# Decode attention on one core: V ahead of the output projection, and eight V rows in small loads

## The chip, the cores and the metric

One NeuronCore of a Trainium2 chip. The metric is the device time of one execution in microseconds, the median of several runs.

## The reference

One token passes through attention over a cache of 65,536 positions and through a gated MLP, and a scalar gate mixes the two:

```python
# x [1,1,512] bf16; k_cache, v_cache [1,32,65536,128] bf16; wq [512,4096]; wo [4096,512]
# w_gate, w_up [512,1792]; w_down [1792,512]; gate_w [512]
q = (x @ wq).reshape(1, 1, 32, 128).transpose(0, 2, 1, 3)
scores = einsum("bhqd,bhkd->bhqk", q, k_cache) * 128 ** -0.5
o = einsum("bhqk,bhkd->bhqd", softmax(scores), v_cache)
a = o.transpose(0, 2, 1, 3).reshape(1, 1, 4096) @ wo
b = (silu(x @ w_gate) * (x @ w_up)) @ w_down
g = sigmoid((x * gate_w).sum(-1, keepdims=True))
return g * a + (1 - g) * b
```

K and V are 537 MB each and are read once. The weights are some 14 MB.

## The kernel before

All loads go into one large buffer, `mem`, of 184 units; a unit is 512 bf16 columns in 128 partitions, 128 KB. A head's 65,536 positions are cut into two halves (z = 0 and 1), and in each half a partition holds 256 consecutive positions, "rows" of 128 elements here. So a half of K or V is 64 units, 8 MB, one DMA. K's halves lie at units 32 to 95 and 0 to 63, V's at 120 to 183 and 96 to 159: they overlap, so a load waits until what it overwrites has been used.

SP issues nearly all loads, in an order written out by hand. Inside its loop over heads: K's first half of head i+2, V's first half of head i+1, K's second half, V's second half. Each waits on one of two counters: `ktdone` counts K pieces that DVE has transposed, `pvdone` the groups of V matmuls that PE has finished.

For a head, DVE transposes K in 16 pieces of 32 rows (L415, L422) into the two buffers of `kt`. PE makes scores from each piece (L472), into `psS`. The maximum of the scores goes through DVE and PE, ACT takes the exponentials into `pa` (L288), and DVE rearranges them into the coefficients `pb` (`shuffle`, L331; signals `s_pba` and `s_pbz` for the two halves). PE then makes four rows of partial sums in `psO` with matmuls of four V rows each, 128x512 (`values`, L525), in four groups per head of 40, 24, 40 and 24 matmuls. ACT scales the four rows into `orow`, and `turn` (L499) adds and turns them into a column in `psT`, which ACT stores in `oTn`. PE runs one head behind: in the loop's iteration i it makes the scores of head i and the values of head i-1. Before, the order in an iteration is: six pieces of K's first half, the first 40 V matmuls, the last two pieces, `turn`, 24 V matmuls, the eight pieces of K's second half, 40 V matmuls, 24 V matmuls.

Behind the loop is the last head's V, in eight loads of `tail`, each entry a place in `mem`, a first row and a number of rows. `piece` (L561) uses every V row as weights, with one column of coefficients, and adds into the column `psW`. The output projection wo is applied in three parts: 31 of its 32 rows per partition (`wo`, loaded ahead of V's tail) by 31 matmuls of 128x512 into `psY` (L576), which already holds the MLP's result; row 31 (`wj`) for the other heads, and the last head's block (`w31`) for the head that has just been finished, both loaded last, by eight matmuls of 128x128 into `psZ` (L600). `psY` reaches `psZ` through `yrow` and `hot` (L584). ACT copies `psZ` to `fin`, and SP and ACT store two of the four output rows each.

The MLP, the gate and q are made at the start, while the first K loads run.

## Time and profile before

| | before |
|---|---|
| median of 3 runs | 2513.8 us (2513.74 to 2513.82) |
| span of the profiled execution | 2512.4 us |
| PE, DVE, ACT busy | 1709.8, 1411.8, 64.6 us |
| bytes read from HBM | 1087.77 MB, 433 GB/s over the span |
| packets on SP's DMA queue | 20452 |

The profile is of one execution. The span runs from its first to its last instruction, and it is the only time that the profile gives of this execution. The median of the runs counts what lies around the span too, 1.4 us more. [...] "SPq" lines are the issues of loads, not the transfers. The waits of a load's consumer tell when it landed.

### The profile page before, as it was taken

The numbers are of one execution on the slowest core, as the hardware profiler recorded it, in microseconds if no ns is written. First come the engines' busy times: TensorE is split into PE (matmuls) and PEld (weight loads), VectorE is DVE, ScalarE is ACT, GpSimd is POOL, SyncE is SP. The second block draws the span as 40 slices with busy tenths as digits, with TensorE's granted clock in tenths as the row PEclk, the third lists the DMA queues.
The fourth block names the chain that finished last, engine by engine and source line by source line (L and its number), as shares of the span: only waits on it lengthen the run. The fifth ranks groups of instructions, "written<-read, shape, count | busy, mean of one in ns | idle before, by whom it ended". The sixth has DMA issues, their size and how long they took to land.

```text
span 2512.4 us, 51694 instructions
## 1 busy us (share of the span) xinstructions
PE 1709.8 (68%) x21624; PEld 978.8 (39%) x21624; DVE 1411.8 (56%) x1683; ACT 64.6 (3%) x195; POOL 0.2 (0%) x4
## 2 busy tenths in 40 slices
PE   4666766667667677676676766766767767677677
PEld 3334433333433344333443333343334333344334
DVE  4764565554655645646456555465564564645653
ACT  0000000000000000000000000000000000000000
POOL 0000000000000000000000000000000000000000
PEclk8667767777677677776776767767767677677677
DMA  9999999999999999999999999999999999999999
GB/s 420 436 434 434 434 435 434 434 434 434 434 434 434 434 434 434 434 434 434 434 434 434 434 434 434 434 434 434 434 434 434 434 434 434 435 434 434 434 435 402
DMA packets 20470, 1087.93 MB, mean 433 GB/s; under 512 B 2282, under 2 KB 2668, under 8 KB 2924
## 3 DMA queue, kind: packets, MB, share of 16 engines
q1 hardware_dynamic: 20452, 1087.78, 100.0%
q8 instruction: 9, 0.15, 0.0%
q14 instruction: 1, 0.01, 0.0%
q10 hardware_dynamic: 8, 0.00, 0.0%
HBM read 1087.77 MB, written 0.00 MB: 433 GB/s over the span
## 4 chain that ended last, share of the span: by engine, by line
DMA 70%; PE 27%; DVE 1%; issue 1%; SPq 0%; ACT 0%; DVEq 0%
DMA mem<-in_A_v_cache_dram 67%; PE psO L525 27%; DMA mem<-in_A_k_cache_dram 2%; DMA mem<-in_A_wo_dram 1%; DVE kt L322 1%; DMA mem<-in_A_wq_dram 0%; DVE kt L415 0%; SPq L224 0%; PE psM L456 0%; DVE pb L331 0%; PE psS L472 0%; PE psM L547 0%; DVE sm L336 0%; PE psZ L600 0%; PE psM L549 0%
## 5 line engine op out<-in xcount | busy, mean ns | idle before, releaser
L472 PE MATMUL psS<-qcur,kt 128*128 128x4 bf16 x16384 | 573.0, 169 | 728.3 <-DVE kt L415 414.2
L525 PE MATMUL psO<-mem,pb 128*4 128x512 bf16 x3968 | 1040.6, 428 | 32.9 <-DMA mem<-in_A_v_cache_dram 32.6
L472 PEld LDWEIGHTS psS<-qcur,kt 128*128 128x128 bf16 x16384 | 534.0, 105 | 791.9 <-issue 789.5
L422 DVE STREAM_TRANSPOSE kt<-mem 128x2048 uint32<-128x2048 uint32 x248 | 547.6, 2275 | 402.3 <-DMA mem<-in_A_k_cache_dram 402.3
L415 DVE STREAM_TRANSPOSE kt<-mem 128x2048 uint32<-128x2048 uint32 x248 | 551.3, 2280 | 240.3 <-DMA mem<-in_A_k_cache_dram 239.3
L525 PEld LDWEIGHTS psO<-mem,pb 128*4 128x4 bf16 x3968 | 359.4, 93 | 657.5 <-issue 238.4
L331 DVE COPY pb<-pa 32x64 bf16<-32x64 bf16 x1024 | 233.5, 228 | 15.1 <-ACT pa L288 1.5
L338 DVE TENSOR_REDUCE sc<-psM 1x1 f32<-1x128 f32 x32 | 8.9, 279 | 334.9 <-PE psM L547 334.9
L336 DVE TENSOR_REDUCE sm<-psS 128x1 f32<-128x512 f32 x32 | 22.1, 692 | 42.3 <-PE psS L472 42.3
L322 DVE STREAM_TRANSPOSE kt<-mem 128x2048 uint32<-128x2048 uint32 x16 | 35.4, 2277 | 17.0 <-DMA mem<-in_A_k_cache_dram 17.0
L286 ACT ACTIVATE sm<-psM 128x1 f32<-128x1 f32 x32 | 5.5, 171 | 1222.7 <-PE psM L549 1222.7
L282 ACT ACTIVATE oTn<-psT,gcol 128x1 f32 (+1 forms) x31 | 8.2, 264 | 1035.1 <-PE psT L499 1035.1
L499 PE MATMUL psT<-ident,orow 4*128 4x1 f32 x256 | 33.5, 248 | 0.5 <-ACT orow L280 0.5
L499 PEld LDWEIGHTS psT<-ident,orow 4*128 4x128 f32 x256 | 30.8, 186 | 1.2 <-ACT orow L280 0.6
L280 ACT ACTIVATE orow<-psO,sm 4x512 f32<-4x512 f32 x31 | 21.0, 677 | 130.3 <-PE psO L525 126.0
L288 ACT ACTIVATE pa<-psS,sm 128x512 bf16<-128x512 f32 x32 | 22.0, 687 | 1.0
L549 PE MATMUL psM<-sc,onesf 1*128 1x1 f32 x64 | 12.3, 259 | 11.9 <-DVE sc L338 11.9
L561 PE MATMUL psW<-pb,mem 128*128 128x1 bf16 x512 | 14.5, 164 | 5.2 <-DMA mem<-in_A_v_cache_dram 4.7
L549 PEld LDWEIGHTS psM<-sc,onesf 1*128 1x128 f32 x64 | 9.6, 186 | 21.5 <-DVE sc L338 21.5
L561 PEld LDWEIGHTS psW<-pb,mem 128*128 128x128 bf16 x512 | 13.9, 100 | 6.4 <-issue 4.2
L553 PEld LDWEIGHTS psM<-sm,onesf 128*128 128x128 f32 x64 | 9.7, 191 | 14.7 <-issue 13.5
L553 PE MATMUL psM<-sm,onesf 128*128 128x1 f32 x64 | 12.5, 264 | 1.1 <-ACT pa L288 1.1
(72 smaller groups left out, 94.0 us busy)
## 6 DMA issues: line engine op xcount, KB each, us to landing
mem<-in_A_v_cache_dram SPq DMA_DIRECT2D x3, 4096.0 KB, 29.4
mem<-in_A_k_cache_dram SPq DMA_DIRECT2D x2, 4096.0 KB, 38.7
mem<-in_A_wq_dram SPq DMA_DIRECT2D x1, 4096.0 KB, 12.3
mem<-in_A_wo_dram SPq DMA_DIRECT2D x1, 3968.0 KB, 36.7
mem<-in_A_v_cache_dram SPq DMA_DIRECT2D x1, 2048.0 KB, 31.2
mem<-in_B_w_gate_dram SPq DMA_DIRECT2D x1, 1792.0 KB, 16.0
mem<-in_B_w_up_dram SPq DMA_DIRECT2D x1, 1792.0 KB, 21.0
mem<-in_B_w_down_dram SPq DMA_DIRECT2D x1, 1792.0 KB, 24.7
```

The lines of the kernel that those rows point to most:

```text
L288: nc.scalar.activation(pa[:], psS[:], ACT.Exp, bias=nbias, scale=SCALE, accum_out=rsum).then_inc(expdone, 1)
L322: nc.vector.transpose(kt[:, i % 2, :].rearrange("p (j r t) -> p r j t", j=2, t=32), src.rearrange("p (r j t) -> p r j t", j=2, t=32)).then ...
L331: last = nc.vector.tensor_copy(dst, sr)
L336: nc.vector.reduce_max(mxs, psS[:], AX_X).then_inc(s_mx, 1)
L415: nc.vector.transpose(kt[:, c % 2, :].rearrange("p (j r t) -> p r j t", j=2, t=32), src.rearrange("p (r j t) -> p r j t", j=2, t=32)).then ...
L422: nc.vector.transpose(kt[:, c % 2, :].rearrange("p (j r t) -> p r j t", j=2, t=32), src.rearrange("p (r j t) -> p r j t", j=2, t=32)).then ...
L472: last = nc.tensor.matmul(psS[:, o:o + 4] if j is None else psS[:, ds(j * (2 * PR) + o, 4)], ktb[b][:, je // 2, r, :, je % 2], qcur[:, je, ...
L499: last = nc.tensor.matmul(psT[:, 0:1], orow[0:4, i * Dh:(i + 1) * Dh], ident[0:4, i:i + 1], start=(i == 0), stop=(i == 3))
L525: last = nc.tensor.matmul(psO[0:4, :], pb[:, k_col[256 * z + r]:k_col[256 * z + r] + 4], vt[:, r * Dh:(r + 4) * Dh], start=(z == 0 and par ...
L549: nc.tensor.matmul(amx, onesf[0:1, :], gm, start=True, stop=True).then_inc(s_ar, 1)
L553: nc.tensor.matmul(Lt, onesf[:], rsum, start=True, stop=True).then_inc(s_L, 1)
L561: last = nc.tensor.matmul(psW[:, 0:1], vt[:, r * Dh:(r + 1) * Dh], pb[:, col:col + 1], start=(r0 + r == 0), stop=(r0 + r == R - 1))
```

## The change

V's tail is issued ahead of wo. It comes in six loads instead of eight, and it no longer waits behind wo: the first goes where K's first half was, and the order of the gates is ktdone less a half, ktdone less 3, ktdone in full, pvdone less 1.

Eight of the 512 rows per partition (112 to 119 of the first half) are left out of `tail`. They come in 16 loads, each of eight partitions, every fourth one, with 2 KB per partition. All are placed in partitions 0 to 63 of two other places (`LO`, `HI`): the data of partitions 0 to 63 in `LO`, that of 64 to 127 in `HI`. For `HI` the coefficients are copied to partitions 0 to 63 (`pbx`). These rows and the first tail load are multiplied four rows at a time into `psO`, as in the loop, and turned into `psW` afterwards.

wo comes last, whole, in five loads of 14, 9, 5, 3 and 1 rows. The last head's column is put into `amat` with the others, so the extra loads `wj` and `w31`, the matmuls L576 and the buffers `hot`, `oR` and `w4` go. Each of wo's 32 rows takes four matmuls of 128x128, one into each of four partitions of `psZ` (0, 32, 64, 96). The MLP's result goes to `psZ` before them. One store by ACT writes the four output rows; SP's store and its wait go.

In PE's loop the eight pieces of K's first half come in one inner loop ahead of the first V matmuls, and `turn` and the next 24 follow directly. The branch `j is None` and the unrolled pair go.

```diff
-    tail = [(32, 0, 128), (0, 128, 128), (V0 + 24, 256, 128), (V0 + 64, 384, 64),
-            (V0 + 80, 448, 32), (V0 + 56, 480, 16), (V0 + 60, 496, 12), (V0 + 63, 508, 4)]
-    WOJ, WO31 = V0, V0 + 1
+    tail = [(64, 0, 112), (30, 120, 136), (0, 256, 120), (V0 + 64, 376, 80), (V0 + 40, 456, 32), (V0 + 48, 488, 24)]
+    HALF = P // 2
+    LO, HI, R8 = 92, 94, 112
+    octs = [slice(q + o, q + o + 29, 4) for q in (0, 32) for o in range(4)]
+    wo_rows = [14, 9, 5, 3, 1]
...
-            sp.wait_ge(ktdone, 2 * NP * H - NP)
-            sp.dma_start(at(WO, 31 * D), w_dram["wo"][:, 0:31 * D]).then_inc(d["wo"], 16)
...
-            need = {0: (ktdone, 2 * NP * H - 4), 1: (ktdone, 2 * NP * H), 2: (pvdone, 4 * H - 1)}
+            need = {0: (ktdone, 2 * NP * H - NP), 1: (ktdone, 2 * NP * H - 3), 2: (ktdone, 2 * NP * H),
+                    3: (pvdone, 4 * H - 1)}
             for n, (kb, r0, nr) in enumerate(tail):
...
+                if n == 0:
+                    for w in octs:
+                        for k8, p0 in ((LO, 0), (HI, HALF)):
+                            sp.dma_start(at(k8, 8 * Dh)[w],
+                                         src[0][p0:p0 + HALF, R8 * Dh:(R8 + 8) * Dh][w]).then_inc(d8, 16)
             sp.wait_ge(pvdone, 4 * H)
-            sp.dma_start(at(WOJ, D), wj_dram).then_inc(d["wj"], 16)
-            sp.dma_start(at(WO31, D), w31_dram).then_inc(d["w31"], 16)
-            sp.wait_ge(s_fin, 1)
-            sp.dma_start(out_dram[2:4, :], fin[32:34, :]).then_inc(s_out2, 16)
+            j0 = 0
+            for n, nj in enumerate(wo_rows):
+                sp.dma_start(at(WO + j0, nj * D), w_dram["wo"][:, j0 * D:(j0 + nj) * D]).then_inc(dw_[n], 16)
+                j0 += nj
...
             shuffle(0, s_pba)
+            dve.wait_ge(s_pba, H)
+            for q in range(0, HALF, 32):
+                last = nc.vector.tensor_copy(pbx[q:q + 32, :], pb[HALF + q:HALF + q + 32, k_col[R8]:k_col[R8] + 8])
+            last.then_inc(s_pbx, 1)
...
+            for q in range(4):
+                w = slice(32 * q, 32 * q + 32)
+                last = nc.vector.tensor_scalar(amat[w, H - 1, q:q + 1], psW[w, 0:1], LiG[w], None, ALU.mult)
             last.then_inc(s_A, 1)
             dve.wait_ge(s_R, 1)
...
+            nc.vector.tensor_copy(w1[:], psQ[:, 0, 0:32]).then_inc(s_w4, 1)
...
-                pieces(0, 0, NP - 2)
+                pieces(0)
                 with nc.tensor.If(i > 0):
...
                     values(0, 0)
-                pieces(0, NP - 2, NP)
-                with nc.tensor.If(i > 0):
-                    turn()
+                    turn().then_inc(s_pt, 1)
                     values(0, 1)
-                pieces(1, 0, NP)
+                pieces(1)
...
+            def eight():
+                pe.wait_ge(d8, 16 * 2 * len(octs))
+                pe.wait_ge(s_pbx, 1)
+                for kb, cf, c0 in ((LO, pb, k_col[R8]), (HI, pbx, 0)):
+                    for r in range(0, 8, 4):
+                        last = nc.tensor.matmul(psO[0:4, :], cf[0:HALF, c0 + r:c0 + r + 4],
+                                                at(kb, 8 * Dh)[0:HALF, r * Dh:(r + 4) * Dh],
+                                                start=False, stop=(kb == HI and r == 4))
+                return last
...
+            piece(0)
+            eight().then_inc(s_v0, 1)
+            piece(1)
...
+            zt = [psZ[32 * c:32 * c + 1, 0:128] for c in range(4)]
...
+            pe.wait_ge(s_or, H + 1)
+            turn(psW, False, False)
+            piece(5).then_inc(s_w, 1)
...
+            for n, nj in enumerate(wo_rows):
+                pe.wait_ge(dw_[n], 16)
+                for j in range(j0, j0 + nj):
+                    for c in range(4):
+                        last = nc.tensor.matmul(zt[c], w1[:, j:j + 1], wo_ap[:, j, c, :], start=False, stop=(j == 31))
+                j0 += nj
             last.then_inc(s_z4, 1)
```

More of the change, by code (lines that the diff above doesn't have):

```diff
@@ L89, in bass_gated_mix__mha_block_cached__swiglu_ffn__decode_kernel @@
         pb = sb("pb", [P, 512], BF16)
+        pbx = sb("pbx", [HALF, 8], BF16)
         orow = sb("orow", [P, 512], F32)
@@ L93, in bass_gated_mix__mha_block_cached__swiglu_ffn__decode_kernel @@
         onesf = sb("onesf", [P, 128], F32)
-        hot = sb("hot", [P, 2, 2], F32)
         sc = sb("sc", [P, 8], F32)
@@ L104, in bass_gated_mix__mha_block_cached__swiglu_ffn__decode_kernel @@
         bmat = sb("bmat", [P, 32], BF16)
-        oR = sb("oR", [P, 32], BF16)
-        w4 = sb("w4", [P, 2, 2, 2], BF16)
+        w1 = sb("w1", [P, 32], BF16)
         fin = sb("fin", [P, 128], BF16)
@@ L119, in bass_gated_mix__mha_block_cached__swiglu_ffn__decode_kernel @@
         gm = sc[0:1, 5:6]
-        names = ("x", "gw", "wq", "wg", "wu", "wd", "ka0", "ka", "kz", "va", "vz", "wo", "wj", "w31")
+        names = ("x", "gw", "wq", "wg", "wu", "wd", "ka0", "ka", "kz", "va", "vz")
         d = {n: sem("d_" + n) for n in names}
         dt_ = [sem(f"d_t{i}") for i in range(len(tail))]
+        d8 = sem("d_8")
+        dw_ = [sem(f"d_w{i}") for i in range(len(wo_rows))]
         s_ones = sem("s_ones")
@@ L130, in bass_gated_mix__mha_block_cached__swiglu_ffn__decode_kernel @@
         s_unit = sem("s_unit")
-        s_hot0 = sem("s_hot0")
-        s_hot = sem("s_hot")
         s_z = sem("s_z")
@@ L160, in bass_gated_mix__mha_block_cached__swiglu_ffn__decode_kernel @@
         s_pbz = sem("s_pbz")
+        s_pbx = sem("s_pbx")
         s_L = sem("s_L")
@@ L167, in bass_gated_mix__mha_block_cached__swiglu_ffn__decode_kernel @@
         s_R = sem("s_R")
-        s_oR = sem("s_oR")
-        s_y = sem("s_y")
         s_yr = sem("s_yr")
         s_w = sem("s_w")
+        s_v0 = sem("s_v0")
         s_w4 = sem("s_w4")
-        s_wj = sem("s_wj")
         s_z4 = sem("s_z4")
@@ L176, in bass_gated_mix__mha_block_cached__swiglu_ffn__decode_kernel @@
         s_zz = sem("s_zz")
-        s_out2 = sem("s_out2")
         s_out = sem("s_out")
@@ L189, in bass_gated_mix__mha_block_cached__swiglu_ffn__decode_kernel @@
         }
-        wj_dram = w_dram["wo"][:, 31 * D:32 * D]
-        w31_dram = A_wo.rearrange("(h d) n -> h d n", d=Dh)[H - 1]
-        WQ, WG, WU, WD, WO = V0, 0, 14, V0 + 64, 64
+        WQ, WG, WU, WD, WO = V0, 0, 14, V0 + 64, V0
         wq_ap = at(WQ, Dc * H * Dh).rearrange("p (c n) -> p c n", c=Dc)
@@ L196, in bass_gated_mix__mha_block_cached__swiglu_ffn__decode_kernel @@
         wd_ap = at(WD, FC * D).rearrange("p (c n) -> p c n", c=FC)
-        wo_ap = at(WO, 32 * D).rearrange("p (j n) -> p j n", j=32)
-        w2_ap = at(WOJ, 2 * D).rearrange("p (e c n) -> p e c n", e=2, c=4)
+        wo_ap = at(WO, 32 * D).rearrange("p (j c n) -> p j c n", j=32, c=4)
         ktb = [kt[:, b, :].bitcast(BF16).rearrange("p (j r m e) -> p j r m e", j=2, r=NG, e=2) for b in range(2)]
@@ L216, in bass_gated_mix__mha_block_cached__swiglu_ffn__decode_kernel @@
         ctx.callback(lambda: nc.scalar.wait_ge(s_out, 16))
-        ctx.callback(lambda: nc.sync.wait_ge(s_out2, 16))
         block = ctx.enter_context(nc.Block())
@@ L298, in _ @@
             row_norm(H - 2)
+            act.wait_ge(s_v0, 1)
+            nc.scalar.copy(orow[0:4, :], psO[0:4, :]).then_inc(s_or, 1)
             act.wait_ge(s_z4, 1)
-            nc.scalar.copy(fin[0:34, :], psZ[0:34, 0:128]).then_inc(s_fin, 1)
+            nc.scalar.copy(fin[0:97, :], psZ[0:97, 0:128]).then_inc(s_fin, 1)
             act.wait_ge(s_fin, 1)
-            act.dma_start(out_dram[0:2, :], fin[0:2, :]).then_inc(s_out, 16)
+            act.dma_start(out_dram, fin[0:97:32, :]).then_inc(s_out, 16)
         @block.vector
@@ L350, in _ @@
             link(nc.vector.memset(amat[:], 0.0))
-            link(nc.vector.memset(w4[:], 0.0))
-            nc.vector.memset(psZ[0:64, 0:128], 0.0).then_inc(s_zz, 1)
-            nc.vector.memset(hot[0:1, :, :], 0.0)
+            nc.vector.memset(psZ[:, 0:128], 0.0).then_inc(s_zz, 1)
             nc.vector.memset(ident[:], 0.0)
@@ L360, in _ @@
             link(last)
-            nc.vector.memset(hot[0:1, :, :].rearrange("p a b -> p (a b)")[:, 0:4:3], 1.0).then_inc(s_hot, 1)
             link(nc.vector.transpose(kt[:, 1, 0:1024], kt[:, 0, 0:1024]))
@@ L433, in _ @@
                 last = nc.vector.tensor_copy(amat[32 * q:32 * q + 32, 0:H - 1, q], oTn[32 * q:32 * q + 32, 0:H - 1])
+            nc.vector.tensor_copy(yrow[0:1, :], psY[0:1, :]).then_inc(s_yr, 1)
+            dve.wait_ge(s_w, 1)
+            for q in range(4):
+                w = slice(32 * q, 32 * q + 32)
+                last = nc.vector.tensor_scalar(amat[w, H - 1, q:q + 1], psW[w, 0:1], LiG[w], None, ALU.mult)
             last.then_inc(s_A, 1)
             dve.wait_ge(s_R, 1)
-            nc.vector.tensor_copy(oR[:], psQ[:, 0, 0:32]).then_inc(s_oR, 1)
-            diag = w4[:].rearrange("p e a b -> p e (a b)")[:, :, 0:4:3]
-            nc.vector.tensor_copy(diag[:, 0, :], psQ[:, 0, 31:32].to_broadcast([P, 2])).then_inc(s_wj, 1)
-            dve.wait_ge(s_y, 1)
-            nc.vector.tensor_copy(yrow[0:1, :], psY[0:1, :]).then_inc(s_yr, 1)
-            dve.wait_ge(s_w, 1)
-            nc.vector.tensor_scalar(diag[:, 1, :], psW[:, 0:1].to_broadcast([P, 2]), LiG, None, ALU.mult).then_inc(s_w4, 1)
+            nc.vector.tensor_copy(w1[:], psQ[:, 0, 0:32]).then_inc(s_w4, 1)
         @block.tensor
@@ L471, in scores @@
                         o = col + PR * b + 4 * r
-                        last = nc.tensor.matmul(psS[:, o:o + 4] if j is None else psS[:, ds(j * (2 * PR) + o, 4)],
+                        last = nc.tensor.matmul(psS[:, ds(j * (2 * PR) + o, 4)],
                                                 ktb[b][:, je // 2, r, :, je % 2],
@@ L492, in _, with turn @@
                 last = nc.tensor.matmul(psY[0:1, :], guT[:, j:j + 1], wd_ap[:, j, :],
-                                        start=(j == 0), stop=False)
+                                        start=(j == 0), stop=(j == FC - 1))
             last.then_inc(s_b, 1)
             pe.wait_ge(s_unit, 1)
-            def turn():
+            def turn(to=psT, first=True, final=True):
                 for i in range(4):
-                    last = nc.tensor.matmul(psT[:, 0:1], orow[0:4, i * Dh:(i + 1) * Dh], ident[0:4, i:i + 1],
-                                            start=(i == 0), stop=(i == 3))
-                last.then_inc(s_pt, 1)
+                    last = nc.tensor.matmul(to[:, 0:1], orow[0:4, i * Dh:(i + 1) * Dh], ident[0:4, i:i + 1],
+                                            start=(first and i == 0), stop=(final and i == 3))
+                return last
             nc.tensor.sem_inc(pvdone, 4)
@@ L510, in pair, with pieces @@
                             pe.wait_ge(s_qc, i + 1)
-                        pe.wait_ge(ktdone, n + (c + b + 1) if j is None else n + j * 2 + (c + b + 1))
+                        pe.wait_ge(ktdone, n + j * 2 + (c + b + 1))
                         scores(b, PR * c, j)
-                def pieces(z, c0, c1):
-                    if c1 - c0 == 2:
-                        pair(NP * z + c0, None)
-                        return
-                    with nc.tensor.Fori(0, (c1 - c0) // 2) as j:
-                        pair(NP * z + c0, j)
+                def pieces(z):
+                    with nc.tensor.Fori(0, NP // 2) as j:
+                        pair(NP * z, j)
                 def values(z, part):
@@ L558, in piece @@
                 vt = at(kb, nr * Dh)
-                for r in range(nr):
+                for r in range(0, nr, 1 if n else 4):
                     col = k_col[r0 + r]
-                    last = nc.tensor.matmul(psW[:, 0:1], vt[:, r * Dh:(r + 1) * Dh], pb[:, col:col + 1],
-                                            start=(r0 + r == 0), stop=(r0 + r == R - 1))
+                    if n == 0:
+                        last = nc.tensor.matmul(psO[0:4, :], pb[:, col:col + 4], vt[:, r * Dh:(r + 4) * Dh],
+                                                start=(r == 0), stop=False)
+                    else:
+                        last = nc.tensor.matmul(psW[:, 0:1], vt[:, r * Dh:(r + 1) * Dh], pb[:, col:col + 1],
+                                                start=(n == 1 and r == 0), stop=(r0 + r == R - 1))
+                return last
+            def eight():
[6 more added lines that the diff above has]
+                                                start=False, stop=(kb == HI and r == 4))
                 return last
             pe.wait_ge(s_or, H)
-            turn()
+            turn().then_inc(s_pt, 1)
             pe.wait_ge(s_pba, H)
             piece(0)
+            eight().then_inc(s_v0, 1)
+            piece(1)
+            pe.wait_ge(s_yr, 1)
+            pe.wait_ge(s_zz, 1)
+            zt = [psZ[32 * c:32 * c + 1, 0:128] for c in range(4)]
+            for c in range(4):
+                nc.tensor.matmul(zt[c], onesf[0:1, 0:1], yrow[0:1, 128 * c:128 * c + 128], start=True, stop=False)
+            pe.wait_ge(s_pbz, H)
+            piece(2)
+            piece(3)
+            piece(4)
+            pe.wait_ge(s_or, H + 1)
+            turn(psW, False, False)
+            piece(5).then_inc(s_w, 1)
             pe.wait_ge(s_A, 1)
@@ L572, in _ @@
                              start=True, stop=True).then_inc(s_R, 1)
-            pe.wait_ge(s_oR, 1)
-            pe.wait_ge(d["wo"], 16)
-            for j in range(31):
-                last = nc.tensor.matmul(psY[0:1, :], oR[:, j:j + 1], wo_ap[:, j, :], start=False, stop=(j == 30))
-            last.then_inc(s_y, 1)
-            piece(1)
-            pe.wait_ge(s_yr, 1)
-            pe.wait_ge(s_hot, 1)
-            pe.wait_ge(s_zz, 1)
-            zt = [psZ[32 * (c // 2):32 * (c // 2) + 2, 0:128] for c in range(4)]
-            for c in (0, 2, 1, 3):
-                nc.tensor.matmul(zt[c], hot[0:1, c % 2, :], yrow[0:1, 128 * c:128 * c + 128],
-                                 start=(c % 2 == 0), stop=False)
-            pe.wait_ge(s_pbz, H)
-            piece(2)
-            piece(3)
-            piece(4)
-            piece(5)
-            piece(6)
-            piece(7).then_inc(s_w, 1)
-            pe.wait_ge(s_wj, 1)
-            pe.wait_ge(d["wj"], 16)
-            for e in range(2):
-                if e == 1:
-                    pe.wait_ge(d["w31"], 16)
-                    pe.wait_ge(s_w4, 1)
-                for c in (0, 2, 1, 3):
-                    last = nc.tensor.matmul(zt[c], w4[:, e, c % 2, :], w2_ap[:, e, c, :], start=False,
-                                            stop=(e == 1 and c % 2 == 1))
+            pe.wait_ge(s_w4, 1)
+            j0 = 0
+            for n, nj in enumerate(wo_rows):
+                pe.wait_ge(dw_[n], 16)
+                for j in range(j0, j0 + nj):
+                    for c in range(4):
+                        last = nc.tensor.matmul(zt[c], w1[:, j:j + 1], wo_ap[:, j, c, :], start=False, stop=(j == 31))
+                j0 += nj
             last.then_inc(s_z4, 1)
```

## The prediction

> **What bounds the kernel now.** I read the page first, then the chain of waits, then the timeline of one head and of the last 35 us, and last the busy time in short windows around the end.

> ```profile
> span 2512.4 us, 51694 instructions
> ...
> DMA  9999999999999999999999999999999999999999
> GB/s 420 436 434 434 434 435 434 434 434 434 434 434 434 434 434 434 434 434 434 434 434 434 434 434 434 434 434 434 434 434 434 434 434 434 435 434 434 434 435 402
> ...
> DMA 70%; PE 27%; DVE 1%; issue 1%; SPq 0%; ACT 0%; DVEq 0%
> ```

> The DMA queues are full in every slice, at 434 GB/s in all but the first and the last. The chain calls 27% of the span PE, but these are stretches in which SP waits for PE before it issues the next V load, while another load is still running. So the time is bytes over 434 GB/s, plus what the two ends add, as long as every load is issued before the one ahead of it runs dry. All times below are set against the profiled span of 2512.4 us; the median of the runs is 2513.8, so 1.4 us lies around the span, and I carry that over unchanged.

> One head, from the timeline (start, length, engine, line):

> ```profile
> 2395.25 0.33 SPq L224 DMA_DIRECT2D mem<-in_A_v_cache_dram  x1
> 2403.36 8.89 DVE L415 STREAM_TRANSPOSE kt<-mem 128x2048 uint32<-128x2048 uint32 x4 [7.76 <-DMA mem<-in_A_k_cache_dram]
> 2416.06 8.89 DVE L415 STREAM_TRANSPOSE kt<-mem 128x2048 uint32<-128x2048 uint32 x4
> 2420.70 1.14 PE L472 MATMUL psS<-qcur,kt 128*128 128x4 bf16 x32 [1.01 <-DVE kt L415]
> 2422.56 10.58 PE L525 MATMUL psO<-mem,pb 128*4 128x512 bf16 x40 [0.72 <-DMA mem<-in_A_v_cache_dram]
> 2433.07 1.75 PE L472 MATMUL psS<-qcur,kt 128*128 128x4 bf16 x64
> 2433.30 0.33 SPq L224 DMA_DIRECT2D mem<-in_A_v_cache_dram  x1
> 2433.85 0.34 SPq L251 DMA_DIRECT2D mem<-in_A_wo_dram  x1
> 2435.73 7.03 PE L525 MATMUL psO<-mem,pb 128*4 128x512 bf16 x24
> 2441.94 17.66 DVE L422 STREAM_TRANSPOSE kt<-mem 128x2048 uint32<-128x2048 uint32 x8 [13.02 <-DMA mem<-in_A_k_cache_dram]
> 2461.26 11.70 PE L525 MATMUL psO<-mem,pb 128*4 128x512 bf16 x40 [0.37 <-DMA mem<-in_A_v_cache_dram]
> ```

> A half of K or V (256 rows per partition, 8 MB) lands every 19.3 us: at 2403.36 (K), 2422.56 (V), 2441.94 (K) and 2461.26 (V), each seen by the engine that waits for it. The V load that lands at 2461.26 was issued at 2433.30, 8.6 us before the K load ahead of it had landed. That 8.6 us is the slack of the loop.

> The end:

> ```profile
> 2480.01 1.05 PE L499 MATMUL psT<-ident,orow 4*128 4x1 f32 x8 [0.51 <-ACT orow L280]
> 2480.99 3.36 PE L561 MATMUL psW<-pb,mem 128*128 128x1 bf16 x128
> 2484.93 8.17 PE L576 MATMUL psY<-mem,oR 128*1 128x512 bf16 x31 [0.28 <-DVE oR L436]
> 2509.33 0.51 PEld L561 LDWEIGHTS psW<-pb,mem 128*128 128x128 bf16 x16 [0.41 <-DMA mem<-in_A_v_cache_dram]
> 2509.97 0.22 DVE L442 TENSOR_SCALAR w<-psW,sm 128x2 bf16<-128x2 f32 x1 [16.15 <-PE psW L561]
> 2510.11 0.60 PE L600 MATMUL psZ<-mem,w 128*2 128x128 bf16 x8 [0.18 <-DMA mem<-in_A_wo_dram]
> 2510.76 0.26 ACT L300 CAST fin<-psZ 34x128 bf16<-34x128 f32 x1 [29.40 <-PE psZ L600]
> 2511.04 0.33 SPq L263 DMA_DIRECT2D out_dram<-fin  x1
> ```

> The last bytes are V's and two late rows of wo. From the last landing (about 2510.1) to the copy of the result are 0.65 us, and then the store. PE waits for DMA, not the reverse.

> Windows near the end; the last two columns are the DMA share and GB/s:

> ```profile
> 2507.50:2508.00 0.50, 0.50 (x25) 0.50 (x22) 0.00 (x0) 0.00 (x0) 0.00 (x0) 0.50 1.07 406
> 2508.50:2509.00 0.50, 0.50 (x16) 0.42 (x16) 0.00 (x0) 0.00 (x0) 0.00 (x0) 0.50 0.60 215
> 2509.00:2509.50 0.50, 0.18 (x7) 0.17 (x7) 0.00 (x0) 0.00 (x0) 0.00 (x0) 0.50 0.59 205
> 2509.50:2510.00 0.50, 0.43 (x16) 0.34 (x13) 0.03 (x1) 0.00 (x0) 0.00 (x0) 0.50 0.38 123
> 2510.00:2510.50 0.50, 0.39 (x8) 0.23 (x8) 0.19 (x1) 0.00 (x0) 0.00 (x0) 0.50 0.00 0
> ```

> The 16 DMA engines do not end together. The share is full until 2508.0, stands at 0.60 for a microsecond, and is 0 after 2510. So six or seven of the 16 have nothing to do for about 1.5 us, and the others set the end. This is what the eight-row loads act on.

> **The change part by part.**

> *Bytes.* V is the same. wo came as 31 rows plus two extra rows (rows 31 twice, in two layouts), 33 x 128 KB; now 32. That is 128 KB less, at 434 GB/s 0.30 us: **-0.3**.

> *Eight-row loads.* The eight tokens are 256 KB, in 16 loads of 16 KB, eight partitions of 2 KB each. Two things are unknown: how many DMA engines share a load of eight rows, and the cost of a small load. For the second the nearest rows are the last two V loads and the first late row of wo:

> ```profile
> 2474.78 0.91 SPq L258 DMA_DIRECT2D mem<-in_A_v_cache_dram  x2
> 2479.22 0.33 SPq L260 DMA_DIRECT2D mem<-in_A_wo_dram  x1
> mem<-in_A_v_cache_dram SPq DMA_DIRECT2D x1, 384.0 KB, 34.5
> mem<-in_A_v_cache_dram SPq DMA_DIRECT2D x1, 128.0 KB, 34.4
> mem<-in_A_wo_dram SPq DMA_DIRECT2D x1, 128.0 KB, 30.8
> ```

> The pair of issues takes 0.91 us, so the second starts 0.48 us after the first, at 2475.26. The 128 KB of V land at 2475.26 + 34.4 = 2509.66, the 128 KB of wo at 2479.22 + 30.8 = 2510.02: 0.36 us apart, where the bytes alone take 0.30. So a small load that stands in a full queue costs 0.06 us over its bytes, with eight packets on each engine; mine have one. Per load I take a third of it, 0.02, in all 0.3; the bounds are 0.1 (an eighth) and 1.0 (16 x 0.06). An engine moves 434/16 = 27.1 GB/s. If a load of eight rows stays on eight engines, each of these carries 32 KB instead of 16, 0.6 us more, with the overhead 0.9 (0.7 to 1.6); the other eight carry 16 KB less, -0.6. What this does to the end hangs on which eight. If they are the ones that are idle after 2508.5, they have 1.5 us of room, and the late ones end 0.6 earlier: -0.6. If late ones are among them, the end moves by +0.9. No row names the engines. I take **-0.6**, since the level of 0.60 over a whole microsecond looks like one fixed group that runs ahead, and eight rows into one half of the partitions are a fixed group too; +0.9 is the other bound, and goes into the range.

> [...]

> *SP's queue.* 16 more issues at up to 0.48 us (the pair above) are 7.7 us of SP. The first tail load waits for the same count of K transposes as the wo load did (2433.85). After the loop's last V load, which moves 3.6 us (below), it is issued at about 2437.5 and the 16 are out by 2445. The next tail load waits for five transposes of K's second half, 2441.94 + 5 x 17.66/8 = 2453.0, so nothing is held up. DMA then still has the V load until 2461.3, and behind it 3584 + 256 KB, 9.1 us, until 2470. The later tail loads are gated as before, on transposes that end at 2459.6 and on V's matmuls at 2473, with 4352 and 3840 KB still ahead of them; wo's are issued where the late rows are now, at 2479.2. Nothing runs dry: 0.

> *The loop.* Only PE's order changes: all eight K pieces come ahead of the first 40 V matmuls, where six did. These 40 no longer start when V lands (2422.56) but after the eighth piece: the transposes end at 2416.06 + 8.89 = 2424.95, its matmuls take 1.14, so 2426.2, 3.6 us later. SP's wait for them queues the V load of the second half and, behind it, K's next. It is issued at 2436.9, 5.0 us ahead of the landing at 2441.94. The nearest row for what a load needs to get going is the first one:

> ```profile
> mem<-in_A_wq_dram SPq DMA_DIRECT2D x1, 4096.0 KB, 12.3
> ```

> 4 MB take 9.7 us at 434 GB/s, so 2.6 us are its start and its landing. 5.0 - 2.6 leaves 2.4 us of cover: 0. The turn of the output row (1.05, from L499), then the other 24 V matmuls, end by 2426.2 + 10.58 + 1.05 + 7.03 = 2444.9, about when the first scores of K's second half can start (2441.94 + 2.2): at most 0.7 us late, and they must end by 2461.26. Also 0.

> *The end.* The rows of three groups (count | busy, mean ns):

> ```profile
> L600 PE MATMUL psZ<-mem,w 128*2 128x128 bf16 x8 | 0.6, 289 | 0.2 <-DMA mem<-in_A_wo_dram 0.2
> L571 PE MATMUL psQ<-bmat,amat 128*128 128x32 bf16 x1 | 0.2, 210 | 0.1
> L436 DVE CAST oR<-psQ 128x32 bf16<-128x32 f32 x1 | 0.2, 191 | 0.3 <-PE psQ L571 0.3
> ```

> Landings, counted from 2461.3 at 434 GB/s: tail pieces of 112 rows and the eight, 2470; 136, 2480.5; 120, 2489.5; 80, 2495.6; 32, 2498.0; 24, 2499.8; then wo's 14, 9, 5, 3 and 1 rows at 2504.0, 2506.7, 2508.2, 2509.1, 2509.4. PE: from 2481.0, 28 wide matmuls of 10.58/40 = 0.26 us, 7.4, and four more of half height, 1.1: 2489.5. The rest of V at 3.36/128 = 0.026 each: 136 until 2493.1, 120 until 2496.2, 80 until 2498.3, 32 until 2499.1, the turn (1.05) 2500.2, the last 24 2500.8. Then four DVE products (0.22 each), one matmul and one copy (0.2 each) and their hand-overs, some 2 us: 2502.8, before wo's first piece lands. DVE's two small copies of coefficients lie near 2483, 18 us ahead of their next use on the path. wo's matmuls: the row of L600 has eight in 0.60 us, the last of them 0.29 long and a wait for DVE in between, so at most 0.3/7 = 43 ns from start to start; four per row are 0.17 us against 0.30 for the row's bytes. PE keeps up and waits for the last row. Behind that are four matmuls where eight stood, and one store where two were issued on two queues: 0 to -0.3, I take **-0.1**.

> Sum: -0.3 - 0.6 - 0.1 = -1.0: span 2511.4, time **2512.8**.

> **The rivals.**

> *The loaded eight are late ones.* -0.3 + 0.9 - 0.1 = +0.5: 2514.3. For it: nothing says which are late. Against: the fixed group above.

> *The eight rows spread over all 16 engines*, so that this part does nothing: -0.3 - 0.1 + 0.1 of overhead: 2513.5.

> *V's load comes too late in each head* (slower). The 2.4 us of cover are used up if the 40 matmuls end over 6.0 us later than now instead of 3.6. The matmuls of L525 vary: 10.58 and 11.70 above. Each microsecond beyond is a hole in the DMA, 30 times: one such microsecond gives 2543. It decides from 0.2 us per head on. Against: 11.70 instead of 10.58 uses only 1.1 of the 2.4.

> *PE becomes the bound in wo.* 128 matmuls at 0.60/8 = 75 ns, waits and all, are 9.6 us from 2504.0 on: 2513.6 instead of 2509.5, +4: 2516.9. Against: in the 0.60 us is the wait.

> *The small loads go one at a time.* From the store's issue at 2511.04 to the end of the span is 1.36 us; 16 such in a row, less the 0.6 of bytes, are +21: 2534. Against: 0.36 us from one small load's landing to the next, above. [...]

> **How the numbers follow.** A measurement of this kernel tells 0.2%, 5 us, from no change. Forecast 0.48 (2512.3 to 2513.2, by the overhead and the last term), spread 0.10, late eight 0.26, PE bound 0.06: all within 5 us, 0.90. V too late 0.05 and one at a time 0.02 are slower by more: 0.07. No row shows 5 us to be gained, since the DMA has no hole; 0.03 for something unseen. The range takes in the first three cases with the overhead's bounds, 2512.3 to 2514.7, 0.84 of the chance.

> **What would show it.** Right: 434 GB/s in all inner slices; V's second load issued about 3.6 us later against K's landing; wo last, its matmuls waiting for DMA; the DMA share dropping to 0 within less than 1 us instead of 1.5. Wrong: slices under 430 in the loop (V too late), wo's matmuls back to back until the end (PE bound), a dip of the DMA share near 2470 (small loads), or a share of about a half for over 2 us at the end (late eight).

## The result, and the profile after

| | before | after |
|---|---|---|
| median | 2513.81 us (2513.74 to 2513.95, 6 runs) | 2531.16 us (2519.31 to 2541.50, 6 runs) |
| ratio, 95% interval | | 1.0069 (1.0050 to 1.0088) |
| profiled execution: time, span | span 2512.4 us | 2535.16 us, span 2533.5 us |

Predicted were 2512.8 us, 2512.3 to 2514.7. The change costs 17 us, and the runs, which lay within 0.2 us of each other, now lie 22 us apart. The page of after:

```profile
span 2533.5 us, 52334 instructions
...
GB/s 419 429 431 429 423 423 438 437 433 429 431 431 433 436 422 430 431 439 436 433 430 431 438 435 433 433 430 426 428 433 433 427 431 435 430 426 428 419 429 385
...
DMA 74%; DVE 14%; issue 9%; PE 2%; SPq 0%; DVEq 0%; ACT 0%
```

The row that stood at 434 to 436 in every inner slice now goes from 419 to 439, 431 on the mean: the loss is in the loop, over the whole span. The chain now has DVE and "issue" in it, where it had DMA and SP's waits for PE.

What SP waited for, in the loads of the loop (total us, times, longest), after:

```profile
SPq L219 <- PE psO L523: 1402.5, 61, 25.5
```

The same row of before:

```profile
SPq L224 <- PE psO L525: 1260.9, 61, 21.5
```

The longest wait grew by 4.0 us. Two such waits per head make up the 61. The one for the 40 matmuls grew by 4.1 us on the mean (from 20.7 to 24.8), the other by only 0.5; together they make the 141.6 us.

The timeline of the last head, which answers to the one of before:

```profile
2422.27 8.89 DVE L413 STREAM_TRANSPOSE kt<-mem 128x2048 uint32<-128x2048 uint32 x4 [8.67 <-DMA mem<-in_A_k_cache_dram]
2431.09 3.86 DVE L332 COPY pb<-pa 32x64 bf16<-32x64 bf16 x16
2434.98 8.89 DVE L413 STREAM_TRANSPOSE kt<-mem 128x2048 uint32<-128x2048 uint32 x4
2445.49 11.05 PE L523 MATMUL psO<-mem,pb 128*4 128x512 bf16 x40 [0.33 <-issue]
2456.71 0.33 SPq L219 DMA_DIRECT2D mem<-in_A_v_cache_dram  x1
2460.91 2.31 DVE L420 STREAM_TRANSPOSE kt<-mem 128x2048 uint32<-128x2048 uint32 x1 [13.05 <-DMA mem<-in_A_k_cache_dram]
2481.37 10.19 PE L523 MATMUL psO<-mem,pb 128*4 128x512 bf16 x40 [1.50 <-DMA mem<-in_A_v_cache_dram]
```

The 40 V matmuls start 23.2 us after K's landing (2445.49 - 2422.27), not 19.2 as before (2422.56 - 2403.36). So V's load is issued at 2456.71, 4.2 us ahead of K's landing, where before it was 8.6. The V half then lands 20.5 us after the K half, not 19.3: 1.2 us are lost. A head of the same execution with a little more lead and no loss:

```profile
1353.81 10.76 PE L523 MATMUL psO<-mem,pb 128*4 128x512 bf16 x40 [0.32 <-issue]
1364.74 0.33 SPq L219 DMA_DIRECT2D mem<-in_A_v_cache_dram  x1
1369.22 17.66 DVE L420 STREAM_TRANSPOSE kt<-mem 128x2048 uint32<-128x2048 uint32 x8 [13.04 <-DMA mem<-in_A_k_cache_dram]
1388.53 1.86 PE L523 MATMUL psO<-mem,pb 128*4 128x512 bf16 x4 [0.35 <-DMA mem<-in_A_v_cache_dram]
```

Here the lead is 4.48 us, and V is seen 19.3 after K. I took this lead (first transpose of K's second half, less SP's issue of the V load) for all 30 heads from the timeline, and beside it the time from this transpose to the same one of the next head, less 77.27, which it is before:

| lead, us | heads | lost per head, mean (highest), us |
|---|---|---|
| over 4.5 | 10 | 0.12 (0.44) |
| 4.0 to 4.5 | 9 | 0.58 (1.65) |
| 3.5 to 4.0 | 10 | 0.94 (1.8) |
| under 3 | 1 | 3.0 |

Together 18.9 us. That is how much later the last head's K is seen (2460.91 against 2441.94, the first ones at 123.80 and 123.73). The median lead is 4.1 us; before it was 8.25 (7.5 to 9.1). The single heads scatter: of the 19 with a lead of 3.5 to 4.5 us some lose nothing and some 1.8 us, and what decides between these stays open. The loss begins well before the load ahead has landed as a whole, and the 16 DMA engines do not finish together: of the landing records of one load, one from each engine, the last comes 1.7 to 1.9 us behind the first in before, and 1.7 to 3.1 us in after.

The packet records of the same traces tell what the engines do in that time. K and V come in packets of 64 KB, which before take 2.418 us each (the longest of the 15,360 in these 30 heads 2.429). After, an engine is without a packet for 4.1 us longer in all (mean of the 16), around the late V load. The larger part of the loss is slow packets: they take 2.432 us on the mean, which makes 13.5 us on each engine, and 10.9 of these lie in packets that start within 6 us behind the issue of the late load. Of the 1,104 packets that start there, 166 take over 0.5 us longer than 2.418, the longest 1.95. So a late load costs mostly by slow packets, and less by empty engines. Why they are slow, no trace here shows.

Behind the last head's K, after needs 2533.5 - 2460.9 = 72.6 us, before 2512.4 - 2441.9 = 70.5: the end is 2.1 us longer, 1.2 of it the loss of the last V half, above. Its last part:

```profile
2523.04 0.91 DVE L440 TENSOR_SCALAR amat<-psW,sm 32x1 bf16<-32x1 f32 x4 [19.31 <-PE psW L561]
2525.65 1.66 PE L603 MATMUL psZ<-mem,w 128*1 128x128 bf16 x56 [1.43 <-DMA mem<-in_A_wo_dram]
2529.92 0.70 PE L603 MATMUL psZ<-mem,w 128*1 128x128 bf16 x20 [0.40 <-DMA mem<-in_A_wo_dram]
2530.86 0.59 PE L603 MATMUL psZ<-mem,w 128*1 128x128 bf16 x16 [0.23 <-DMA mem<-in_A_wo_dram]
2531.80 0.61 ACTq L303 DMA_DIRECT2D out_dram<-fin  x1
```

PE waits for wo and takes 1.66/56 = 30 ns per matmul. The windows (the last two columns are the DMA share and GB/s):

```profile
2528.00:2528.50 0.50, 0.10 (x8) 0.10 (x12) 0.00 (x0) 0.00 (x0) 0.00 (x0) 0.50 0.69 266
2528.50:2529.00 0.50, 0.50 (x26) 0.50 (x22) 0.00 (x0) 0.00 (x0) 0.00 (x0) 0.50 0.32 123
2529.50:2530.00 0.50, 0.10 (x12) 0.08 (x12) 0.00 (x0) 0.00 (x0) 0.00 (x0) 0.50 0.18 74
2530.50:2531.00 0.50, 0.27 (x16) 0.14 (x12) 0.00 (x0) 0.00 (x0) 0.00 (x0) 0.50 0.07 23
```

The share doesn't drop within a microsecond; it tails off over two and a half, at the end with one engine of 16 (0.07). Theory: the loop's order delays each V load, and the engines that finish early run dry. Rival: the eight-row loads, or the new end, cost the time.

### The profile page after: what moved, and what is told of

The parts are those of the page before. It is cut to its first block, busy times and chain, and to the rows that moved or that the text cites. A ratio compares the mean times of both kernels' runs of the same rounds, so it can differ in the third digit from the quotient of the medians.

```text
span 2533.5 us, 52334 instructions
## 1 busy us (share of the span) xinstructions
PE 1702.7 (67%) x21633; PEld 995.5 (39%) x21633; DVE 1412.9 (56%) x1684; ACT 65.2 (3%) x196; POOL 0.2 (0%) x4
## 2 busy tenths in 40 slices
DMA  9999999999999999999999999999999999999999
DMA packets 20726, 1087.80 MB, mean 429 GB/s; under 512 B 2410, under 2 KB 2540, under 8 KB 3052
## 4 chain that ended last, share of the span: by engine, by line
DMA 74%; DVE 14%; issue 9%; PE 2%; SPq 0%; DVEq 0%; ACT 0%
DMA mem<-in_A_k_cache_dram 71%; DVE kt L413 7%; DVE kt L420 6%; PE psO L523 2%; DMA mem<-in_A_wo_dram 1%; DMA mem<-in_A_v_cache_dram 1%; DVE kt L323 1%; DMA mem<-in_A_wq_dram 0%; DVE pb L332 0%; SPq L219 0%; PE psS L473 0%; PE psM L457 0%; DVEq L418 0%; DVEq L411 0%; SPq L261 0%
## 5 line engine op out<-in xcount | busy, mean ns | idle before, releaser
L473 PE MATMUL psS<-qcur,kt 128*128 128x4 bf16 x16384 | 597.6, 170 | 749.6 <-DVE kt L413 478.5
L523 PE MATMUL psO<-mem,pb 128*4 128x512 bf16 x3968 | 1006.3, 418 | 37.8 <-DMA mem<-in_A_v_cache_dram 27.5
L473 PEld LDWEIGHTS psS<-qcur,kt 128*128 128x128 bf16 x16384 | 556.2, 106 | 804.7 <-issue 804.5
L523 PEld LDWEIGHTS psO<-mem,pb 128*4 128x4 bf16 x3968 | 353.0, 91 | 634.5 <-issue 201.0
L500 PEld LDWEIGHTS psT<-ident,orow 4*128 4x128 f32 x256 | 30.8, 186 | 14.1 <-issue 13.5
L545 PE MATMUL psM<-sc,onesf 1*128 1x1 f32 x64 | 12.3, 259 | 11.9 <-DVE sc L339 11.9
L545 PEld LDWEIGHTS psM<-sc,onesf 1*128 1x128 f32 x64 | 9.6, 186 | 21.5 <-DVE sc L339 21.5
L549 PEld LDWEIGHTS psM<-sm,onesf 128*128 128x128 f32 x64 | 9.7, 191 | 14.7 <-issue 13.5
L561 PE MATMUL psW<-pb,mem 128*128 128x1 bf16 x392 | 11.1, 164 | 3.2 <-DMA mem<-in_A_v_cache_dram 2.0
L549 PE MATMUL psM<-sm,onesf 128*128 128x1 f32 x64 | 12.4, 264 | 1.1 <-ACT pa L287 1.1
L543 PE MATMUL psM<-ident,sm 128*1 128x128 f32 x64 | 12.4, 276 | 0.8 <-DVE sm L337 0.8
## 6 DMA issues: line engine op xcount, KB each, us to landing
mem<-in_A_k_cache_dram SPq DMA_DIRECT2D x2, 4096.0 KB, 38.7
mem<-in_A_wq_dram SPq DMA_DIRECT2D x1, 4096.0 KB, 12.1
```

What stands on the lines that cost most here:

```text
L473: last = nc.tensor.matmul(psS[:, ds(j * (2 * PR) + o, 4)], ktb[b][:, je // 2, r, :, je % 2], qcur[:, je, :], start=(je == 0), stop=(je == 3))
L500: last = nc.tensor.matmul(to[:, 0:1], orow[0:4, i * Dh:(i + 1) * Dh], ident[0:4, i:i + 1], start=(first and i == 0), stop=(final and i == 3))
L523: last = nc.tensor.matmul(psO[0:4, :], pb[:, k_col[256 * z + r]:k_col[256 * z + r] + 4], vt[:, r * Dh:(r + 4) * Dh], start=(z == 0 and par ...
L545: nc.tensor.matmul(amx, onesf[0:1, :], gm, start=True, stop=True).then_inc(s_ar, 1)
L549: nc.tensor.matmul(Lt, onesf[:], rsum, start=True, stop=True).then_inc(s_L, 1)
```

## The experiments

Times are medians; each kernel has runs of before beside it on the same chip (2513.83 to 2513.87, 19 to 33 runs).

**The loop back, in after.**

```diff
-                pieces(0)
+                pieces(0, 0, NP - 2)
                 with nc.tensor.If(i > 0):
                     values(0, 0)
+                pieces(0, NP - 2, NP)
+                with nc.tensor.If(i > 0):
                     turn().then_inc(s_pt, 1)
                     values(0, 1)
```

> The changed kernel with PE's loop put back as it was (six pieces of K, 40 V matmuls, two pieces); the end stays changed. Theory (the V load of the second half is issued 4 us later and the DMA runs dry in some heads): the loop's part, 18 us of the profiled 21, goes; 2513.5 to 2516, and steady between runs. Rival (the eight-row loads and wo in last place cost it): it stays near 2530 and scatters.

2515.63 us (2515.45 to 2517.21, 10 runs), ratio 1.0008 (0.9998 to 1.0018). The page, and SP's waits:

```profile
GB/s 419 435 434 434 434 435 435 434 434 434 434 434 434 434 434 435 437 436 434 436 434 435 434 434 434 435 434 434 434 434 435 434 434 434 434 434 434 435 434 389
```

```profile
SPq L219 <- PE psO L526: 1261.1, 61, 21.5
```

434 is back, and the wait is the one of before. The loop's order is 15.5 of the 17.4 us; 1.8 us stay with the end.

**The new loop alone, in before.**

```diff
-                pieces(0, 0, NP - 2)
+                pieces(0, 0, NP)
...
-                pieces(0, NP - 2, NP)
```

> The kernel before with only PE's loop changed: all eight pieces of K ahead of the 40 V matmuls; its end stays. Theory: 2520 to 2540, scattering from run to run by several us. Rival (the end costs it): 2513.8, as before.

2530.13 us (2526.93 to 2534.29, 4 runs), ratio 1.0070 (1.0053 to 1.0087). SP's waits in this kernel:

```profile
SPq L224 <- PE psO L525: 1395.0, 61, 25.5
```

The order alone brings the loss, the long wait and the scatter. With the first run this shows the cause from both sides.

**One piece less ahead, in before**: seven K pieces ahead of the 40 matmuls.

```diff
-                pieces(0, 0, NP - 2)
+                pieces(0, 0, NP - 2)
+                pe.wait_ge(ktdone, n + NP - 1)
+                scores(0, PR * (NP - 2), None)
...
-                pieces(0, NP - 2, NP)
+                pe.wait_ge(ktdone, n + NP)
+                scores(1, PR * (NP - 2), None)
```

> The kernel before with seven pieces of K ahead of the 40 V matmuls, where it has six and the changed loop eight. Theory (what counts is how long before the landing of K's second half the V load is issued, and about 2 us are needed): the load is issued 1.8 us later than before, 4 to 5.5 us ahead of the landing, the DMA stays full: 2513.8 to 2514.0, steady. Rival (any delay of these 40 matmuls is passed on, or the changed order costs in another way): a half of the loop's loss, 2520 or more.

2513.80 us (2513.71 to 2514.48, 10 runs), ratio 1.0000 (0.9991 to 1.0010). Its last head:

```profile
2423.82 11.29 PE L525 MATMUL psO<-mem,pb 128*4 128x512 bf16 x40
2435.27 0.33 SPq L224 DMA_DIRECT2D mem<-in_A_v_cache_dram  x1
2442.04 17.66 DVE L422 STREAM_TRANSPOSE kt<-mem 128x2048 uint32<-128x2048 uint32 x8 [13.06 <-DMA mem<-in_A_k_cache_dram]
```

Leads of 5.9 to 8.0 us cost nothing. So some delay is free: nothing is lost down to 5.9 us, 0.12 us per head on the mean from 5.3 to 4.5, and 0.6 to 3 us on the mean below.

**The lead given back by another way**: after, with DVE's shuffle of the first half ahead of K's transposes rather than between the fourth and the fifth.

```diff
+                dve.wait_ge(expdone, i)
+                dve.wait_ge(pvdone, v - 2)
+                shuffle(0, s_pba)
                 dve.wait_ge(d["ka"], dma + 16)
...
-                    if c == NP // 2:
-                        dve.wait_ge(expdone, i)
-                        dve.wait_ge(pvdone, v - 2)
-                        shuffle(0, s_pba)
```

> The changed kernel as it is, with DVE's 16 copies of the first half's coefficients moved ahead of the four first transposes of the head, into DVE's idle time before K lands. The eight pieces are then done 3.9 us earlier. Theory: the V load goes out 6 us or more ahead of K's landing, as before, and the loop's 18 us go: 2514.5 to 2517, steady, as with the loop put back. Rival (the loss lies in the order of PE's work itself, not in when its 40 matmuls start): 2525 or more.

2518.58 us (2517.76 to 2519.46, 10 runs), ratio 1.0019 (1.0009 to 1.0028). Last head:

```profile
2400.41 3.90 DVE L332 COPY pb<-pa 32x64 bf16<-32x64 bf16 x16 [1.58 <-ACT pa L287]
2436.55 0.33 SPq L219 DMA_DIRECT2D mem<-in_A_v_cache_dram  x1
2445.22 4.50 DVE L419 STREAM_TRANSPOSE kt<-mem 128x2048 uint32<-128x2048 uint32 x2 [16.95 <-DMA mem<-in_A_k_cache_dram]
```

PE's order is after's, the lead is 8.7 us again, and the loss is gone in all heads but the first. There two loads come late (their leads to the first engine's landing are 1.3 and 0.9 us), which costs some 3 us once: 2445.22 against 2441.94. That first head is why the time lies above the expectation. So it is the lead that counts, not the order as such.

**After without the eight-row loads**: the first tail load has 120 rows, `eight` and `pbx` go.

```diff
-    tail = [(64, 0, 112), (30, 120, 136), (0, 256, 120), ...
+    tail = [(64, 0, 120), (30, 120, 136), (0, 256, 120), ...
```

> The changed kernel with the new loop, but the eight rows in the ordinary load. Theory: the loop's loss stays, 2518 to 2540 and scattering; the eight rows' 1 to 2 us drown in it. Rival (the small loads cost it): 2513 to 2515.

2531.49 us (2530.39 to 2535.45, 4 runs), ratio 1.0075 (1.0058 to 1.0092): as after. The eight-row loads are not the cause.

**Neither**: this edit, and the loop back.

> The changed kernel with the loop put back and the eight rows in an ordinary load with the 112 ahead of them (120 rows in all 128 partitions). What is left of the change is V ahead of wo, wo whole and in five loads, one store. Theory: 0.3 to 1 us faster than before, 2512.8 to 2513.5, and 1 to 2 us faster than with the eight-row loads. Rival (V ahead of wo itself costs something): 2514.5 or more.

2515.17 us (10 runs), ratio 1.0003 (0.9994 to 1.0013), above the expectation, in two clusters: four runs at 2513.82 to 2514.27, six at 2515.11 to 2515.50. The profiled one (2515.11) is of the upper cluster; in its timeline, and in the DMA queues between 2508.9 and 2510.4 (packets, MB, share):

```profile
2508.71 0.70 PE L598 MATMUL psZ<-mem,w 128*1 128x128 bf16 x20 [0.40 <-DMA mem<-in_A_wo_dram]
2511.01 0.60 PE L598 MATMUL psZ<-mem,w 128*1 128x128 bf16 x16 [1.60 <-DMA mem<-in_A_wo_dram]
```

```profile
q8 instruction: 1, 0.02, 4.0%
```

A packet of 16 KB on the instruction queue, which I read as a fetch of PE's program, takes 0.04 x 16 x 1.5 = 0.96 us of one engine in that window (0.88 to 0.97 us in the traces of before and after, once 1.29 us), and I put it on a late engine: 15 of the 16 landings of wo's last load are in by 2509.91, the last comes at 2511.24. PE stands idle for 1.60 us ahead of the last 16 matmuls. That the place of the last fetch decides between the clusters is read from profiles, and no run moved a fetch alone: the kernel of the next run was profiled at the lower level (2513.82), with its last fetch at 2509.84, and there the 16 landings of wo's last load lie between 2508.16 and 2509.99, none of them late. Against the run with the loop back, wo's last load shows what the eight-row loads do: there its landings go from 2507.69 to 2511.51, here (the one behind the fetch aside) from 2508.11 to 2509.91. The early engines are 0.4 us earlier, the last is 1.6 later.

**A shorter end**: the kernel with neither, with the first 64 rows of the second tail load multiplied four rows at a time (96 fewer PE instructions).

```diff
+    WIDE = 64
...
+                wide = (nr, WIDE)[n] if n < 2 else 0
+                for r in range(0, wide, 4):
+                    col = k_col[r0 + r]
+                    last = nc.tensor.matmul(psO[0:4, :], pb[:, col:col + 4], vt[:, r * Dh:(r + 4) * Dh], ...
```

> As the run without eight-row loads and with the loop put back, but 64 more V rows are multiplied four at a time, which takes 96 instructions out of PE's program behind the loop. Theory (the fourth fetch of PE's instructions, at 2508.97, falls on a DMA engine that still has bytes of wo to bring, and holds them up by 1.3 us in most runs): that fetch goes, and the upper of the two clusters of times, 2515.2, with it: 2513.0 to 2513.9. Rival (V ahead of wo costs 1.3 us for another reason): 2515.2 in most runs.

2514.66 us (2513.80 to 2515.29, 11 runs), ratio 1.0003 (0.9994 to 1.0012): 0.5 better, and the expectation met by a few runs only. There are still four fetches at the end.

**128 such rows, and two stores**: `WIDE = 128`, and SP stores two of the four rows again.

```diff
-            act.dma_start(out_dram, fin[0:97:32, :])
+            act.dma_start(out_dram[0:2, :], fin[0:33:32, :])
...
+            sp.dma_start(out_dram[2:4, :], fin[64:97:32, :])
```

> The best of what has been seen: the loop as before, no eight-row loads, V ahead of wo, 128 of the first 136 rows behind the first load multiplied four at a time (192 PE instructions fewer than one at a time), and the result stored by two issues on two queues, as before. Theory (the single store of four rows takes 0.35 us longer than two of two rows, and the last fetch of instructions holds up a late DMA engine): 2513.2 to 2513.6, 0.3 us under the kernel before. Rival (the fetch still falls before the last bytes): two clusters, the upper near 2514.8.

2514.08 us (2513.76 to 2514.44, 11 runs), ratio 1.0001 (0.9992 to 1.0010): no upper cluster, with 8 packets of 16 KB on the instruction queue instead of 9, so three fetches at the end instead of four, but no run within the expectation either. The stores did not get cheaper:

```profile
2510.73 0.63 SPq L262 DMA_DIRECT2D out_dram<-fin  x1
2510.74 0.60 ACTq L303 DMA_DIRECT2D out_dram<-fin  x1
```

Before, the two issues took 0.33 and 0.26 us, with each pair of rows in neighbouring partitions; with rows 32 partitions apart an issue takes 0.6, for two rows as for four.

**The eight rows in loads of 16 partitions**: loop back, and 8 loads instead of 16.

```diff
-    octs = [slice(q + o, q + o + 29, 4) for q in (0, 32) for o in range(4)]
+    octs = [slice(o, o + 16) for o in range(0, P, 16)]
```

> The changed kernel with the loop put back, and the eight rows in 8 loads of sixteen partitions in place of 16 loads of eight. The bytes are the same. Theory (a load of eight partitions stays on eight DMA engines, and each of its packets costs an engine some 0.15 us instead of 0.075): with sixteen partitions all 16 engines take part, each with 8 packets, so every engine is held up by about 1.2 us instead of eight by 2.4; the step from the landing of the first tail load to that of the second is the same on all engines, and the time is 2515.2 to 2516. Rival (small loads spread over all engines in any case): the steps look as in the run with the loop put back, with two groups 2 us apart.

2516.54 us (2515.23 to 2519.13, 10 runs), ratio 1.0011 (1.0002 to 1.0021), above the expectation and 0.9 more than with eight-row loads. Of this the small loads need not be the cause: in the profiled run (2516.63) 15 of the 16 landings of wo's last load are in by 2511.37 and the last comes at 2512.44, as behind the fetch above; here a fetch starts at 2509.82.

Without small loads (the kernel with neither), the next tail load's landings follow the first tail load's by 10.3 us. With eight rows (the loop back) it is 10.3 us from the earliest to the earliest and 12.4 from the latest to the latest; with sixteen rows it is 11.2 to 12.0 in all 16 places. The semaphore of the small loads says the same: for the 16 loads of eight rows it has 16 updates just behind the issues and then 128, eight for each load, for the 8 loads of sixteen rows 128, sixteen for each. So each load of eight rows has eight landing records, which I read as eight engines, and either way the small loads hold up their engines for longer than their bytes: 2.1 us against 1.2 with eight rows, 0.9 to 1.7 against 0.6 with sixteen.

**All the mends**: after with the early shuffle, no eight-row loads and the shorter end.

> The changed kernel with the early copies of coefficients, without eight-row loads, and with the 96 PE instructions fewer. Theory: 2513.0 to 2514.0, at or slightly under the kernel before. Rival (the new loop costs in another way): over 2516.

2517.26 us (2516.55 to 2518.28, 11 runs), ratio 1.0014 (1.0005 to 1.0023). The time is past the rival's bound, but by the late loads of the first head, which cost 4.4 us here; no later head loses more than 0.13 us.

**A warmer clock**: the 40 matmuls take 10.1 to 11.7 us in after. The granted clock rises within them: in the head shown above, whose 40 start at 1353.81, it is 0.50 until 1357 and 1.00 from 1358. Eight matmuls of 128 columns per K piece, which nothing reads, were to raise it earlier.

```diff
+                for _ in range(8):
+                    nc.tensor.matmul(psQ[0:32, 1, :], bmat[:], amat[:].rearrange("p h q -> p (h q)"), start=True, stop=True)
```

> The changed kernel with eight more small matmuls (128x32 weights, 128 columns, into an unused part of psQ, added work that nothing reads) behind the scores of each piece of K's first half, to keep PE's granted clock up. Theory (the 40 V matmuls take 10.1 to 11.7 us as they start at half clock, and the scatter of the time comes from where the clock's step falls): they take about 8.7 us, the V load goes out 1.5 to 2.5 us earlier, and the loop loses little: 2515.5 to 2521. Rival (PE's clock has no part): 2528 or more, since PE does more work ahead of them.

2534.04 us (2533.75 to 2534.46, 4 runs), ratio 1.0080 (1.0065 to 1.0096). A window ahead of the 40 matmuls (granted clock in the third column from the right):

```profile
1415.00:1420.00 5.00, 4.90 (x105) 4.35 (x102) 4.94 (x7) 0.00 (x0) 0.00 (x0) 0.50 1.06 459
```

PE was busy for 4.90 of 5.00 us and the clock stayed at 0.50, so this did not do what it was for. The four runs lie only 0.7 us apart, where the six of after lie 22 apart; why is not shown. That the clock makes the scatter remains an argument from the group's length.

No kernel here is faster than before.

## Why the prediction was wrong

**The loop: wrong, and the step that failed is "5.0 - 2.6 leaves 2.4 us of cover: 0".** The mechanism stood among the rivals ("V's load comes too late in each head"), at 0.05, and the changed kernel showed the sign named for it, slices under 430. Three terms of the cover were mis-sized. The delay was put at 3.6 us and was 4.0 (23.2 - 19.2). The issue was read from one head with a short group of 40, 10.58 us and 8.6 of lead, while the leads before go down to 7.5 and the prediction's own row had 11.70: 1.1 us. It set this 1.1 against the 2.4 as a rival of its own, never together with the others. The 2.6 us of start and landing were set against the last landing, seen by DVE, though the first engines are done at least 1.7 us earlier; the prediction had read this spread in the end window (0.60 for a microsecond) and used it only there. 2.4 - 0.4 - 1.1 - 1.7 is below 0: no cover in the heads with a short lead, some in those with a long one, as the table by lead shows on the mean. And the rival's price, 30 us for each microsecond, was right in kind: 18.9 us over 30 heads are 0.63 each. What it called a hole is, by the packet records above, 4.1 us of engines without a packet and for the larger part slow packets.

**Bytes: right.** Without the eight-row loads the last landing, the fetch aside, is 2509.91, against 2510.27 before: -0.36, predicted -0.3.

**Eight-row loads: wrong in sign, and hidden by the loop.** -0.6 was taken, with +0.9 as the other bound, on the guess that the eight are a fixed group that runs ahead; no row or run names its engines, and the last landing moves by +1.6, so late engines are among the eight. The rival "the loaded eight are late ones" was the right one of the two, though its sign, a share of about a half for over 2 us, did not show: in the kernel with the loop back only two of the 16 landings of wo's last load come after 2511. What was mis-sized is the cost of a small load in a queue: 0.02 us over its bytes was taken, with 0.06 as the bound. In the landing records of after, the last ones of the small loads follow one another by 0.19 us, against 0.08 for their bytes, but the delay that they leave to the next load is smaller: 12.4 - 10.3 = 2.1 us on a loaded engine, 0.13 for each of the 16, some 0.055 over the bytes. That is 1.5 us more than the 0.6 of bytes spread evenly, near the upper bound of the prediction (1.6) and near the measured +1.6. The row's 0.06 was the right size as it stood; taking a third of it, because its loads had eight packets on each engine, was wrong. That a load of eight partitions goes to eight engines, a supposition of the prediction, is borne out by the landing records: eight for each, against sixteen for a load of sixteen partitions. Nor do the small loads go one at a time, which would have been +21: they hold up a loaded engine by 2.1 us.

**SP's queue: right in effect.** In the kernel with the loop back the 16 issues take 10.78 us instead of 7.7, and nothing waits for it:

```profile
2434.18 10.78 SPq L256 DMA_DIRECT2D mem<-in_A_v_cache_dram  x16
```

**The end.** PE keeps up in wo, as predicted: 28 to 30 ns per matmul against the bound of 43. Unhindered, in the kernel with the shorter end, 128 take 3.58 us:

```profile
2506.74 3.58 PE L602 MATMUL psZ<-mem,w 128*1 128x128 bf16 x128 [0.28 <-DVE w L435]
```

The end was put at -0.1, for fewer matmuls and one store less, but the store is dearer: its issue takes 0.61 us instead of 0.33, and from the issue to the end of the span it takes 2533.5 - 2531.8 = 1.7 us instead of 1.36, some +0.35. The packet of 16 KB that I read as a fetch, behind which the last landing came up to 1.3 us late (the kernel with neither), was in no term. Together, for the kernel with the loop back: -0.36 + 1.6 + 0.35 = +1.6; measured +1.8.

## What to carry to other kernels

A full DMA queue, here at 434 GB/s, did not tell how near it was to running dry (a median lead of 4.1 us instead of 8.25 cost 15.5 us): take from the timeline how long ahead of the landing each load is issued, and compare it with the landing of the first of the 16 engines and with the longest of the groups that gate it. The change of PE's order moved the waits of SP that hang on it (the longest from 21.5 to 25.5 us), and an estimate of the cover has to take the bad end of each term, since a late load came once per head here, for 0.63 us on the mean. Small loads of eight partitions cost more than their bytes here, 0.13 us against 0.08 a piece, and the issue of a store from partitions 32 apart more than one from neighbouring partitions, 0.6 us against 0.3.
